# Softmax in an attention and MoE kernel on one Trainium2 core: chunked exponentials with the maximum as bias, and a new order at the start and in the pairs

## The chip, the cores and the metric

One core of one Trainium2 chip runs the whole program. The metric is the device time of one execution in microseconds (us). The engines are PE (TensorE matmul; PEld are its weight loads), DVE (VectorE), ACT (ScalarE), POOL (GpSimd) and SP (SyncE, which issues all the DMAs here). Each engine works through its own instructions strictly in the order in which they were issued, and waits on semaphores for the others.

## The reference

```python
# q, k, v: (8, 8, 576, 64); attention within chunks of 64 rows
scores = scale * np.matmul(q_c, k_c.transpose(0, 1, 2, 4, 3))      # scale = 1/8
scores = scores - np.max(scores, axis=-1, keepdims=True)
attn = np.exp(scores)
attn = attn / (np.sum(attn, axis=-1, keepdims=True) + 1e-09)
x = (attn @ v_c)  # put together as (4608 tokens, 512)
h = x @ w_in                                # 512 -> 2048
g = h * np.clip(h + 3.0, 0.0, 6.0) / 6.0
out = g @ w_out                             # 2048 -> 512
```

Everything is float32.

## The kernel before

**Blocks.** The 4608 tokens are nine blocks of NT = 512. Attention of a block is two objects `Attention(n, dp)`, each with four heads, laid out as tiles of 128 partitions by 2 x 8 x 64: sixteen pieces of 64 scores a row. `scores` are 64x64 matmuls into two PSUM banks (tile `two`). `soft` has five steps: 0 the row maximum (DVE, L172), 1 the subtraction of it from the scores (DVE, L174, PSUM to SBUF tile `e`), 2 the exponential over the whole tile (ACT, L176), 3 the row sum, the 1e-9 and the reciprocal (DVE, L178, L182, L183), 4 the normalisation (DVE, L185). `turn` transposes on PE, `turned` copies back (ACT, L202), `multiply` is the product with v (PE, L216), `multiplied` writes x (ACT, L228 or L233), and for the first three blocks DVE takes the low half (L234).

**Precision.** Each float32 product is three passes (L246 to L248) over a high and a low half of each operand. Weights come as 64-bit words, and each of sixteen weight tiles is converted: `u` (ACT, L105) from the high words, `r` (ACT, L106) from the low ones, a shift (DVE, L108) and an addition (DVE, L109), then the high half (ACT, L114, a cast) and the low half (DVE, L116).

**Stages.** First, block 0: its two attentions `b0` and `b1` are written out by hand among warm-up matmuls and the first conversions; b0's scores come in two halves `k` of four chunks. `part` are the twelve matmuls of block 0's first tile of h, in pieces. Then a loop over the sixteen tiles `ft` of block 0 converts tile ft + 2 while PE does `mm1(0, ft)` and `mm2` of two tiles earlier. Blocks 1 and 2 run the same way with converted weights. In this stage a table of slots, two per `ft`, places attention steps of later blocks.

**Pairs.** The other six blocks go in three pairs by a scheme with seven instead of eight block products. A pair has 112 slots of six 128x512 matmuls: 56 of the first product (eight columns p of seven products i in the order 1, 5, 6, 7, 2, 3, 4) and 56 of the second. After a slot's matmuls `tick` runs what `todo` holds for it, in order of rank: additions (L597), the gate (ReLU on ACT, L608, then DVE, L609), splits of operands into halves (`units`, `more`; ACT L446, DVE L447), attention steps of the next pair (`put_steady`). POOL does the two subtractions of each column (L617). Products 2, 3 and 4 go on accumulating in the PSUM banks of 1, 5 and 7, after the additions have read them.

What is issued when is an order written out by hand: the instructions of each engine stand in the order in which the Python code calls them.

Of the kernel before, what the change touches and what calls it, by code (L numbers as in the profile page):

```python
# [8 lines left out]
F32 = mybir.dt.float32  # L9
# [8 lines left out]
P = 128  # L18
# [21 lines left out]
FREE = 4 * NFT + 2 * (NFP + LAG + 1)  # L40


@with_exitstack
def tile_kernel(ctx: ExitStack, tc: tile.TileContext, qk_in, v_in, weights, out):
# [54 lines left out]
    def convert(ft, low_on):  # L99


        u = wsc.tile([P, 1024], I32, name="u")
        r = wsc.tile([P, 1024], I32, name="r")
        lo, hi = words[ft][:, :, 0], words[ft][:, :, 1]
        ACT.activation(out=u.bitcast(F32), in_=hi.bitcast(F32), func=AF.Prelu, scale=2.0 ** -112, alpha=2.0 ** 32)  # L105
        ACT.activation(out=r, in_=lo.bitcast(U32), func=AF.Copy, scale=2.0 ** -29)  # L106
        yield
        DVE.tensor_scalar(out=u, in0=u, scalar1=3, scalar2=None, op0=ALU.logical_shift_left)  # L108
        DVE.tensor_tensor(out=u, in0=u, in1=r, op=ALU.add)  # L109
        yield  # L110
        a = u.bitcast(F32).rearrange("p (m t) -> p m t", m=2)
        w[ft] = w_tile(ft, F32R)
        w_h[ft], w_l[ft] = w[ft][:, 0], w[ft][:, 1]
        ACT.copy(out=w_h[ft], in_=a)  # L114
        yield
        low_on.tensor_tensor(out=w_l[ft], in0=a, in1=w_h[ft].bitcast(F32), op=ALU.subtract)  # L116
        yield
# [4 lines left out]
    class Attention:  # L122
# [38 lines left out]
        def soft(self, step, k=None, a=None):  # L161

            every = slice(None)
            if k is None and a is None:
                flat, each = lambda t: t.rearrange("p a c t -> p (a c) t"), lambda t: t.rearrange("p a c -> p (a c)")
                src = step < 2 and flat(self.s)
            else:
                flat = each = lambda t: t[:, every if a is None else a, every if k is None else CHUNKS[k]]
                src = step < 2 and self.part[k]
# [3 lines left out]
            elif step == 1:  # L173
                DVE.tensor_tensor(out=flat(self.e), in0=src, in1=wide(self.m), op=ALU.subtract)  # L174
            elif step == 2:
                ACT.activation(out=flat(self.e), in_=flat(self.e), func=AF.Exp, scale=SCALE)  # L176
# [127 lines left out]
    with tc.tile_pool(name="ps_b", bufs=2, space=bass.MemoryType.PSUM) as ps_b:  # L304
        b0, b1 = [Attention(0, dp, lambda step, dp=dp: two_banks(ps_a if (dp, step) == (0, "o") else ps_b)) for dp in range(NDP)]
        b0.load_qk(parts=2)
        b1.load_qk(raw.tile([P, 2, 2, NB // 2, 2 * CH], F32, name="x"))
        b0.load_v()
        load_w(0)
        load_w(1)  # L310
        b1.load_v(gp.tile([P, 2, NB // 2, 2 * CH], F32, name="g"))
        a1[0].load_qk()
        load_w(2)
        load_w(3)

        c0, c1 = convert(0, DVE), convert(1, DVE)
# [26 lines left out]
        next(c0)  # L343
        warm_up(IDLE[4])
        b1.soft(3)
        next(c0)
        for a in range(2):
            b1.soft(4, a=slice(a, a + 1))
            b1.turn([a])
        finish()  # L350
        next(c1)
        h = ps_h.tile([P, NT], F32, name="h")

        def part(ct, which):
            o = slice(ct * P, (ct + 1) * P)
            x = xs[0, ct // 2][:, :, ct % 2]
            for k in which:
                PE.matmul(h, lhsT=(w_l if k == 2 else w_h)[0][:, 0, o], rhs=x[:, k % 2], start=ct == 0 and k == 0, stop=ct == 3 and k == 2)

        part(0, (0, 1))  # L360
        part(1, (0, 1))
        b1.turned([0])
        b1.turned([1])
        next(c1)
        next(c0)
        b1.multiply([0])
        b1.multiply([1])
        a1[0].scores()
        part(0, (2,))
        part(1, (2,))  # L370
        b1.multiplied([0])
        b1.multiplied([1])
        finish()
        next(c1)
        for k in range(3):
            part(2, (k,))
            part(3, (k,))
        next(c1)
# [151 lines left out]
    for ft in range(NFT):  # L530
# [5 lines left out]
        c = convert(ft + 2, DVE) if ft + 2 < NFT else None  # L536
        if c:
            next(c)
            next(c)
# [5 lines left out]
        if c:  # L545
            next(c)
            next(c)
# [41 lines left out]
    def at(slot, *f, rank=0):  # L589

        todo.setdefault(slot, []).extend((rank, g) for g in f)
# [7 lines left out]
    def put_steady(n, dp, at_):  # L599
        a = Attention(n, dp)  # L600
# [10 lines left out]
    def first_product(s, base, box):  # L611
# [3 lines left out]
        for p in range(NFP):  # L615
# [3 lines left out]
            for k, i in enumerate(ORDER_A):  # L619
# [18 lines left out]
                elif i == 7:  # L638
# [3 lines left out]
                    at(slot + 2, gate)  # L642
                elif i == 2:
                    at(slot + 1, *gated(gq(0, 0), ps))
                elif i in (3, 4):
# [3 lines left out]
                    at(slot + 2, gate)  # L649
                    if i == 3:  # L650
                        at(slot + 2, sub(out, out, gq(0, 0)), sub(t2[p // 2][:, p % 2], gq(1, 1), out))
# [69 lines left out]
    for s in range(NSUP):  # L721
        base = 2 * SLOTS * s
        if s + 1 < NSUP:
            for k in range(2 * NDP):
                put_steady(NSTD + 2 * s + 2 + k // 2, k % 2, base + (6, 23, 40, 78)[k])
# [7 lines left out]
        for k in range(4 * 7):  # L733
            at(base + SLOTS - 5 + int(1.75 * k), lambda k=k, unit=unit: unit(k), rank=1)
        if s + 1 < NSUP:
# [5 lines left out]
            for k in range(7):  # L741
                at(base + SLOTS + 44 + 2 * k, more, rank=1)
# [32 lines left out]
```

## Time and profile before

| | |
|---|---|
| median of 3 runs | 809.25 us (809.24 to 809.95) |
| profiled execution | 809.08 us |
| its span, first to last instruction | 807.2 us |
| granted TensorE clock | 0.999 |
| POOL busy | 65.0 us (8%) |
| DMA | 172.85 MB, mean 214 GB/s |
| chain that ended last | PE 86%, DVE 7%, ACT 4%, DMA 1% |

A profile row of the timeline has the start in us from the start of the span, the duration in us, engine, line, operation, output and inputs, shapes and the count of merged instructions; in brackets the engine's idle time before it and what ended that. A row of the groups has the shapes and count, then total busy us and mean ns of one, then idle us before it. Line numbers are those of the kernel before.

### The profile page before, as it was taken

The page shows a single profiled execution, that of the slowest core. Times are in us where ns is not written, and L with a number is a line of the kernel's source. Part 1 is how long each engine was busy: PE and PEld are TensorE (multiplying, and loading weights), DVE is VectorE, ACT ScalarE, POOL GpSimd, SP SyncE. Part 2 cuts the span into 40 slices and gives each one's busy share as a digit, 9 for nine tenths or more (in the row PEclk, how much of TensorE's full clock was granted, in tenths as well). Part 3 has the DMA queues.
Part 4 walks back from the last instruction along what each step waited for, and adds up shares of the span by engine and source line. Part 5 has one row for each costly group of instructions (what it writes and reads, how often), then busy time and mean ns, then how long its engine had stood idle before and what let it go on. Part 6 is the DMA issues. An engine that isn't in the chain of part 4 may idle for free.

```text
span 807.2 us, 13704 instructions
## 1 busy us (share of the span) xinstructions
PE 796.4 (99%) x5684; PEld 650.0 (81%) x5684; DVE 601.9 (75%) x771; ACT 366.9 (45%) x464; POOL 65.0 (8%) x55
## 2 busy tenths in 40 slices
PE   8999999999999999999999999999999999999997
PEld 5777888888888888888788888888788888888886
DVE  6889867897788682867888776778897856668941
ACT  5878644442453353344473433444634423347330
POOL 0000000000000000222110001222100012221000
PEclk9999999999999999999999999999999999999999
DMA  9980102968888753566556577665566665555463
GB/s 356 410 355 27 53 2 79 310 217 264 291 273 269 246 179 123 203 250 234 179 201 240 207 224 285 252 234 181 201 239 229 214 207 194 205 201 199 176 241 115
DMA packets 50157, 172.85 MB, mean 214 GB/s; under 512 B 4656, under 2 KB 16944, under 8 KB 39472
## 3 DMA queue, kind: packets, MB, share of 16 engines
q1 hardware_dynamic: 50096, 171.99, 60.3%
q8 instruction: 45, 0.74, 0.4%
q14 instruction: 16, 0.13, 0.0%
HBM read 133.17 MB, written 38.80 MB: 213 GB/s over the span
## 4 chain that ended last, share of the span: by engine, by line
PE 86%; DVE 7%; ACT 4%; DMA 1%; issue 1%; SPq 0%; DVEq 0%; ACTq 0%
PE acc L246 19%; PE acc L248 18%; PE acc L247 18%; PE h L246 8%; PE h L248 8%; PE h L247 8%; PE two L216 2%; PE two L154 2%; PE two L198 2%; DMA w<-w_in_out 1%; DVE u L109 1%; DVE u L597 1%; DVE g L609 1%; ACT r L106 1%; ACT u L105 1%
## 5 line engine op out<-in xcount | busy, mean ns | idle before, releaser
L246 PE MATMUL acc<-xop,ws 128*128 128x512 f32 x528 | 208.7, 395 | 0.5
L248 PE MATMUL acc<-xop,ws 128*128 128x512 f32 x528 | 205.7, 390 | 0.0
L247 PE MATMUL acc<-xop,ws 128*128 128x512 f32 x528 | 205.7, 390 | 0.0
L246 PEld LDWEIGHTS acc<-xop,ws 128*128 128x128 f32 x528 | 99.1, 188 | 24.2 <-DVE h L597 2.1
L248 PEld LDWEIGHTS acc<-xop,ws 128*128 128x128 f32 x528 | 99.1, 188 | 20.7
L247 PEld LDWEIGHTS acc<-xop,ws 128*128 128x128 f32 x528 | 99.2, 188 | 19.7
L447 DVE TENSOR_TENSOR xop<-g,xop 128x1024 fp32r<-128x1024 f32 x72 | 87.7, 1238 | 22.5 <-ACT xop L446 22.4
L446 ACT CAST xop<-g 128x1024 fp32r<-128x1024 f32 x72 | 73.2, 1051 | 38.7 <-PE acc L248 21.6
L617 POOL TENSOR_TENSOR g<-g 128x512 f32<-128x512 f32 x24 | 31.0, 1291 | 665.9 <-DVE g L609 665.9
L608 ACT ACTIVATE r<-acc,half 128x512 f32<-128x512 f32 x72 | 49.4, 686 | 71.9 <-DVE acc L597 71.9
L246 PE MATMUL acc<-g,w 128*128 128x512 f32 x192 | 76.3, 397 | 0.0
L246 PE MATMUL h<-x,w 128*128 128x512 f32 x188 | 74.2, 395 | 0.7 <-ACT w L114 0.7
L248 PE MATMUL acc<-g,w 128*128 128x512 f32 x192 | 74.9, 390 | 0.0
L247 PE MATMUL acc<-g,w 128*128 128x512 f32 x192 | 74.8, 390 | 0.0
L248 PE MATMUL h<-x,w 128*128 128x512 f32 x188 | 73.6, 391 | 1.2 <-DVE w L116 1.2
L247 PE MATMUL h<-x,w 128*128 128x512 f32 x188 | 73.2, 390 | 0.0
L609 DVE SCALAR_TENSOR_TENSOR g<-r,acc 128x512 f32<-128x512 f32 x72 | 49.0, 681 | 31.0 <-ACT r L608 31.0
L263 DVE SCALAR_TENSOR_TENSOR r<-r,h 128x512 f32<-128x512 f32 x48 | 32.7, 681 | 32.5 <-ACT r L262 32.5
L246 PE MATMUL h<-xop,ws 128*128 128x512 f32 x144 | 56.2, 391 | 0.0
L247 PE MATMUL h<-xop,ws 128*128 128x512 f32 x144 | 56.0, 389 | 0.0
L248 PE MATMUL h<-xop,ws 128*128 128x512 f32 x144 | 56.0, 389 | 0.0
L262 ACT ACTIVATE r<-h,half 128x512 f32<-128x512 f32 x48 | 32.8, 683 | 47.0 <-PE h L248 47.0
(86 smaller groups left out, 1163.9 us busy)
## 6 DMA issues: line engine op xcount, KB each, us to landing
ws<-b SPq DMA_DIRECT2D x42, 1024.0 KB, 4.8
ws<-a SPq DMA_DIRECT2D x24, 1024.0 KB, 4.9
ws<-a SPq DMA_DIRECT2D x24, 768.0 KB, 4.2
w<-w_in_out SPq DMA_DIRECT2D x16, 1024.0 KB, 18.0
qk<-qk_in SPq DMA_DIRECT2D x16, 1024.0 KB, 6.9
v<-v_in SPq DMA_DIRECT2D x17, 512.0 KB, 5.3
out_t<-o SPq DMA_DIRECT2D x32, 256.0 KB, 3.8
a<-hl SPq DMA_DIRECT2D x32, 256.0 KB, 3.0
```

Source lines behind the costliest of these rows:

```text
L154: PE.matmul(t[o, a, c if k is None else c % 4, :], lhsT=self.qk[rows, c // 4, 0, c % 4, o], rhs=self.qk[rows, c // 4, 1, c % 4, o], start= ...
L198: PE.transpose(out=self.tp[:, a, i], in_=self.e[:, a, 2 * i:2 * i + 2].rearrange("p c t -> p (c t)"), identity=ident)
L246: PE.matmul(ps, lhsT=a_h, rhs=b_h, start=first, stop=False, skip_group_check=more)
L247: PE.matmul(ps, lhsT=a_h, rhs=b_l, start=False, stop=False, skip_group_check=more)
L248: PE.matmul(ps, lhsT=a_l, rhs=b_h, start=False, stop=last, skip_group_check=more)
L262: ACT.activation(out=r, in_=h, func=AF.Relu, bias=half, scale=1.0 / 6.0)
L263: DVE.scalar_tensor_tensor(out=r, in0=r, scalar=1.0, in1=h, op0=ALU.min, op1=ALU.mult)
L446: ACT.copy(out=t[:, :, 0], in_=src)
L447: DVE.tensor_tensor(out=t[:, :, 1], in0=src, in1=t[:, :, 0].bitcast(F32), op=ALU.subtract)
L608: return (lambda: ACT.activation(out=r, in_=ps, func=AF.Relu, bias=half, scale=1.0 / 6.0), lambda: DVE.scalar_tensor_tensor(out=out, in0=r ...
L609: lambda: DVE.scalar_tensor_tensor(out=out, in0=r, scalar=1.0, in1=ps, op0=ALU.min, op1=ALU.mult))
L617: sub = lambda o, x, y: lambda: POOL.tensor_tensor(out=o, in0=x, in1=y, op=ALU.subtract)
```

## The change

The subtraction goes away. Step 1 of `soft` now multiplies the row maxima by -1/8 (ACT, 128x16 or 128x8 numbers), and step 2 is one ACTIVATE of 128x64 per chunk, straight from PSUM, with the column of negated maxima as the bias: sixteen where there was one, eight for each half of b0. At the start the first weight tile is loaded ahead of b0's v, the third ahead of block 1's q and k; a class `Convert` lets the six steps of a conversion be placed one by one; the low words of tile 0 are taken by POOL; and the steps, the pieces of `part` and block 1's scores come in another order. In the pairs, slots get fractional numbers: the whole part says after which slot, the fraction the rank. Attention steps of the pairs are given by a table instead of fixed distances, and the gates of products 7, 3 and 4 and POOL's subtractions get rank 0.1, behind the additions of rank 0. The slots of `units` and `more` are the same as before.

```diff
+STEADY = ((0.6, 6.6, 6.6, 7.5, 8.5, 12.5, 15.5, 17.6, 19.6), ..., (32.6, 38.6, 38.6, 39.5, 40.5, 44.5, 47.5, 49.6, 51.6), ...)
...
+        def words(self):
+            self.r = wsc.tile([P, 1024], I32, name="r")
+            lo = words[self.ft][:, :, 0].bitcast(U32)
+            if self.words_on:
+                self.words_on.tensor_scalar(out=self.r, in0=lo, scalar1=2.0 ** -29, scalar2=None, op0=ALU.mult)
+            else:
+                ACT.activation(out=self.r, in_=lo, func=AF.Copy, scale=2.0 ** -29)
...
             elif step == 1:
-                DVE.tensor_tensor(out=flat(self.e), in0=src, in1=wide(self.m), op=ALU.subtract)
+                ACT.mul(out=each(self.m), in_=each(self.m), mul=-SCALE)
             elif step == 2:
-                ACT.activation(out=flat(self.e), in_=flat(self.e), func=AF.Exp, scale=SCALE)
+                for i in range(2):
+                    for c in range(NB)[every if k is None else CHUNKS[k]]:
+                        s = self.s[:, i, c] if k is None else self.part[k][:, i, c - NB // 2 * k]
+                        ACT.activation(out=self.e[:, i, c], in_=s, func=AF.Exp, bias=self.m[:, i, c:c + 1], scale=SCALE)
...
+        load_w(0)
         b0.load_v()
-        load_w(0)
         load_w(1)
         b1.load_v(gp.tile([P, 2, NB // 2, 2 * CH], F32, name="g"))
+        load_w(2)
         a1[0].load_qk()
-        load_w(2)
         load_w(3)
-        c0, c1 = convert(0, DVE), convert(1, DVE)
+        c0, c1, c2 = Convert(0, POOL), Convert(1), Convert(2)
...
-        next(c0)
         for a in range(2):
             b0.soft(4, a=slice(a, a + 1))
             b0.turn([a])
+        c0.high()
+        c0.words()
+        b1.soft(0)
+        b1.soft(1)
+        c0.shift()
+        c0.add()
         warm_up(IDLE[3])
+        b1.soft(2)
         b0.turned([0])
         b0.turned([1])
         b0.multiply([0])
         b0.multiply([1])
-        b1.soft(0)
-        b1.soft(1)
-        b1.soft(2)
+        warm_up(IDLE[4])
+        c0.cast()
...
     def at(slot, *f, rank=0):
-        todo.setdefault(slot, []).extend((rank, g) for g in f)
+        todo.setdefault(int(slot // 1), []).extend((slot % 1 + rank, g) for g in f)
...
-        for k, f in ((-6, a.load_qk), (0, a.load_v), (0, a.scores), (1, a.tiles), (1, lambda: a.soft(0)), (2, lambda: a.soft(1)), (2, lambda: a.soft(2)), (8, lambda: a.soft(3)),
-                     (9, lambda: a.soft(4)), (12, a.transpose), (15, a.values)):
-            at(at_ + k, f, rank=2)
+        steps = (a.load_qk, a.load_v, lambda: (a.scores(), a.tiles()), soft(0), lambda: (a.soft(1), a.soft(2)), soft(3), soft(4), a.transpose, a.values)
+        for f, t in zip(steps, slots):
+            at(base + t, f)
...
                     at(slot + 1, add(acc[6], ps, u4), relu)
-                    at(slot + 2, gate)
+                    at(slot + 2, gate, rank=.1)
```

Where it moves instructions, first ACT at the start, from b0's exponentials on. In the rows `e` and `g` are the softmax tiles of b0 and b1, `two` a PSUM tile, `w` and `u` the weights. Before:

```order
L176 ACTIVATE e<-e 128x2x256 x2
L105 ACTIVATE u<-w_129 128x1024
L106 ACTIVATE r<-w_129 128x1024
L202 COPY e<-two 128x512 x2
L176 ACTIVATE g<-g 128x1024
L233 CAST x<-two 128x2x4x64 x2
L114 CAST w_349<-u 128x1024
L105 ACTIVATE u<-w_131 128x1024
```

ACT in the same place now:

```order
L192 ACTIVATE m<-m 128x2x4
L197 ACTIVATE e<-two,m 128x64 x8
L192 ACTIVATE m<-m 128x2x4
L197 ACTIVATE e<-two,m 128x64 x8
L112 ACTIVATE u<-w_127 128x1024
L192 ACTIVATE m<-m 128x16
L197 ACTIVATE g<-two,m 128x64 x16
L223 COPY e<-two 128x512 x2
L132 CAST w_372<-u 128x1024
L254 CAST x<-two 128x2x4x64 x2
L112 ACTIVATE u<-w_131 128x1024
```

b1's exponentials now stand ahead of the copy of b0's transposed tile, the cast of the first weights stands ahead of b0's x, and the low words (L106) are gone from ACT.

The second place is ACT in the conversion loop, at block 1's first attention (`r<-h` is the gate's ReLU). Before:

```order
L105 ACTIVATE u<-w_472 128x1024
L106 ACTIVATE r<-w_472 128x1024
L176 ACTIVATE e<-e 128x1024
L262 ACTIVATE r<-h,half 128x512
L114 CAST w_717<-u 128x1024
```

ACT in that place now:

```order
L112 ACTIVATE u<-w_506 128x1024
L120 ACTIVATE r<-w_506 128x1024
L192 ACTIVATE m<-m 128x16
L197 ACTIVATE e<-two,m 128x64 x16
L283 ACTIVATE r<-h,half 128x512
L132 CAST w_761<-u 128x1024
```

One exponential became a product and sixteen exponentials in the same place; what stands ahead and behind is the same.

The third place is DVE in the first pair, in the last two columns of the first product, from column p = 6 on (`u2`, `u4`, `h`, `acc` are additions, `g3` gates, `xop` splits, z and e attention's row sum and normalisation). Before, from that column's first addition:

```order
L597 TENSOR_TENSOR u2_3898<-h_3891,p1_3874 128x512
L597 TENSOR_TENSOR u4_3899<-acc_3882,u2_3898 128x512
L597 TENSOR_TENSOR h_3891<-acc_3900,u4_3899 128x512
L609 SCALAR_TENSOR_TENSOR g3_3206<-r_3909,h_3891 128x512
L609 SCALAR_TENSOR_TENSOR g3_3206<-r_3918,acc_3867 128x512
L597 TENSOR_TENSOR acc_3882<-acc_3882,u2_3898 128x512
L178 TENSOR_REDUCE z_3864<-e_3865 128x16
L182 TENSOR_SCALAR z_3864<-z_3864 128x16
L183 RECIPROCAL z_3864<-z_3864 128x16
L609 SCALAR_TENSOR_TENSOR g3_3206<-r_3927,acc_3882 128x512
L597 TENSOR_TENSOR acc_3900<-acc_3900,u2_3898 128x512
L185 TENSOR_TENSOR e_3865<-e_3865,z_3864 128x1024
```

DVE from the row sum on, now:

```order
L199 TENSOR_REDUCE z_4013<-e_4014 128x16
L203 TENSOR_SCALAR z_4013<-z_4013 128x16
L204 RECIPROCAL z_4013<-z_4013 128x16
L632 TENSOR_TENSOR u2_4092<-h_4085,p1_4070 128x512
L632 TENSOR_TENSOR u4_4093<-acc_4076,u2_4092 128x512
L632 TENSOR_TENSOR h_4085<-acc_4097,u4_4093 128x512
L645 SCALAR_TENSOR_TENSOR g3_3355<-r_4115,acc_4063 128x512
L645 SCALAR_TENSOR_TENSOR g3_3355<-r_4106,h_4085 128x512
L206 TENSOR_TENSOR e_4014<-e_4014,z_4013 128x1024
L632 TENSOR_TENSOR acc_4076<-acc_4076,u2_4092 128x512
L632 TENSOR_TENSOR acc_4097<-acc_4097,u2_4092 128x512
L645 SCALAR_TENSOR_TENSOR g3_3355<-r_4124,acc_4076 128x512
```

The row sum moved from behind the column's first accumulator addition to ahead of its first addition, and the two accumulator additions now stand together ahead of their gates.

More of the change, by code (lines that the diff above doesn't have):

```diff
@@ L97, in load_w, with __init__, high, shift @@
         words[ft] = t.rearrange("p (n t) -> p n t", t=2)
[L99 to L117, printed above, removed]
+    class Convert:
+        def __init__(self, ft, words_on=None):
+            self.ft, self.words_on = ft, words_on
+        def high(self):
+            self.u = wsc.tile([P, 1024], I32, name="u")
+            hi = words[self.ft][:, :, 1]
+            ACT.activation(out=self.u.bitcast(F32), in_=hi.bitcast(F32), func=AF.Prelu, scale=2.0 ** -112, alpha=2.0 ** 32)
+        def words(self):
[5 more added lines that the diff above has]
+                ACT.activation(out=self.r, in_=lo, func=AF.Copy, scale=2.0 ** -29)
+        def shift(self):
+            DVE.tensor_scalar(out=self.u, in0=self.u, scalar1=3, scalar2=None, op0=ALU.logical_shift_left)
+        def add(self):
+            DVE.tensor_tensor(out=self.u, in0=self.u, in1=self.r, op=ALU.add)
+        def cast(self):
+            self.a = self.u.bitcast(F32).rearrange("p (m t) -> p m t", m=2)
+            t = w[self.ft] = w_tile(self.ft, F32R)
+            w_h[self.ft], w_l[self.ft] = t[:, 0], t[:, 1]
+            ACT.copy(out=t[:, 0], in_=self.a)
+        def low(self):
+            DVE.tensor_tensor(out=w_l[self.ft], in0=self.a, in1=w_h[self.ft].bitcast(F32), op=ALU.subtract)
     def two_banks(p):
@@ L349, in tile_kernel, with part @@
             b1.turn([a])
+        c0.low()
         finish()
-        next(c1)
+        b1.turned([0])
+        b1.turned([1])
+        c1.shift()
+        c1.add()
+        c2.high()
+        c2.shift()
         h = ps_h.tile([P, NT], F32, name="h")
-        def part(ct, which):
+        def part(ct, k):
             o = slice(ct * P, (ct + 1) * P)
             x = xs[0, ct // 2][:, :, ct % 2]
[L357 to L365, printed above, removed]
+            PE.matmul(h, lhsT=(w_l if k == 2 else w_h)[0][:, 0, o], rhs=x[:, k % 2], start=ct == 0 and k == 0, stop=ct == 3 and k == 1)
+        for k in (0, 2):
+            part(0, k)
+            part(1, k)
         b1.multiply([0])
         b1.multiply([1])
-        a1[0].scores()
-        part(0, (2,))
-        part(1, (2,))
         b1.multiplied([0])
         b1.multiplied([1])
+        c1.cast()
         finish()
[L374 to L378, printed above, removed]
+        c1.low()
+        c2.words()
+        part(0, 1)
+        part(1, 1)
+        for k in (0, 2, 1):
+            part(2, k)
+            part(3, k)
+            if k == 2:
+                a1[0].scores()
     ps_o = pool("ps_o", 4, space=bass.MemoryType.PSUM)
@@ L535, in tile_kernel @@
         over = []
[L536 to L539, printed above, removed]
+        c = None
+        if ft + 2 < NFT:
+            c = Convert(ft + 2) if ft else c2
+            if ft:
+                c.high()
+                c.words()
+                c.shift()
+            c.add()
         gt = gate(h)
@@ L545, in tile_kernel @@
         if c:
-            next(c)
-            next(c)
+            c.cast()
+            c.low()
         if len(pending) >= LAG:
@@ L731, in unit @@
             next(box["units"])
-        for k in range(4 * 7):
-            at(base + SLOTS - 5 + int(1.75 * k), lambda k=k, unit=unit: unit(k), rank=1)
+        for k, t in enumerate(UNITS):
+            at(base + SLOTS + t, lambda k=k, unit=unit: unit(k))
         if s + 1 < NSUP:
@@ L739, in more @@
                 next(box["x"])
-            for k in range(7):
-                at(base + SLOTS + 44 + 2 * k, more, rank=1)
+            for t in MORE:
+                at(base + SLOTS + t, more)
         first_product(s, base, box)
```

24 lines of the change are left out of this document (14 added, 10 removed).

## Prediction

> **What bounds the kernel now.** I read the page first, then the stretches, then the timeline of each engine where TensorE is not full.
>
> ```profile
> PE 796.4 (99%) x5684; PEld 650.0 (81%) x5684; DVE 601.9 (75%) x771; ACT 366.9 (45%) x464; POOL 65.0 (8%) x55
> ```
> ```profile
> 10.00:20.00 10.00, 9.22 (x140) 7.68 (x134) 9.43 (x15) 7.33 (x10) 0.00 (x0) 1.00 1.02 412
> 100.00:200.00 100.00, 100.00 (x804) 82.20 (x803) 76.62 (x119) 42.14 (x58) 0.00 (x0) 1.00 0.54 172
> ```
> Behind the time in a row of the stretches stand busy us of PE, PEld, DVE, ACT and POOL, the clock, the DMA share and GB/s. From 100 to 200 us TensorE is busy throughout at clock 1.00, and no matmul is removed by the change. So DVE and ACT time is worth nothing by itself; the change can win or lose only where TensorE waits for them. The timeline of PE shows three such places: the first 33 us, the conversion of the weights up to 65 us, and the last column of each pair's first product.
>
> **The start.** The other engines' rows there:
>
> ```profile
> 6.30 0.69 DVE L172 TENSOR_REDUCE m<-two 128x8 f32<-128x512 f32 x1 [5.44 <-PE two L154]
> 8.96 1.46 DVE L178 TENSOR_REDUCE z<-e 128x8 f32<-128x512 f32 x2
> 10.95 1.29 DVE L185 TENSOR_TENSOR e<-e,z 128x512 f32<-128x512 f32 x2
> 12.16 1.22 DVE L172 TENSOR_REDUCE m<-two 128x16 f32<-128x1024 f32 x1
> ```
> ```profile
> 12.66 1.14 ACT L105 ACTIVATE u<-w 128x1024 f32<-128x1024 f32 x1 [2.96 <-DMA w<-w_in_out]
> 14.76 1.05 ACT L202 COPY e<-two 128x512 f32<-128x512 f32 x2
> 28.46 1.05 ACT L114 CAST w<-u 128x1024 fp32r<-128x1024 f32 x1 [1.03 <-DVE u L109]
> 29.93 1.13 ACT L105 ACTIVATE u<-w 128x1024 f32<-128x1024 f32 x1
> ```
> The first weights land at 12.66. Moved ahead of b0's v (0.5 MB, at 412 GB/s 1.3 us) they land near 11.4; v then lands near 12.7 and is needed only after the copy that stood at 14.76, so it costs nothing. The third weights change places with block 1's q and k (1 MB each, 2.6 us): those then land about when the third weights did, some 22 us, and their scores stand behind b1's product with v, later than 25 us here. b1's scores now wait for b0's first eight exponentials to leave their PSUM bank, 9.0 instead of about 8.9, ahead of warm-up matmuls that nothing needs: no cost.
>
> The price that decides is one exponential of 128x64 with a pointer as bias, out of PSUM. No row has it. The nearest:
>
> ```profile
> L608 ACT ACTIVATE r<-acc,half 128x512 f32<-128x512 f32 x72 | 49.4, 686 | 71.9 <-DVE acc L597 71.9
> L202 ACT COPY e<-two 128x1024 f32<-128x1024 f32 x16 | 16.2, 1011 | 22.5 <-PE two L198 22.4
> L202 ACT COPY e<-two 128x512 f32<-128x512 f32 x2 | 1.0, 574 | 0.0
> L74 ACT ACTIVATE warm<-half 128x1 f32<-128x1 f32 x1 | 0.2, 203 | 0.0
> ```
> ```profile
> 387.27 0.69 ACT L608 ACTIVATE r<-h,half 128x512 f32<-128x512 f32 x1 [2.90 <-DVE h L597]
> 387.86 0.68 ACT L608 ACTIVATE r<-acc,half 128x512 f32<-128x512 f32 x1
> ```
> An element costs (1011 - 574)/512 = 0.85 ns. The gate's ReLU has the same operands (PSUM in, pointer bias): 686 - 448 x 0.85 = 305 ns for 64 columns, and 387.27 to 387.86 shows that the next starts 0.59 after it, 0.59 - 0.38 = 0.21 for 64. I take 0.20 from start to start. Ends: 0.31 (no overlap) and 0.10 (574 ns copies follow each other by 1.05 - 0.57 = 0.48, so 0.48 - 0.38). The multiplication of the maxima by -1/8 is 0.21 by the 128x1 row, and 0.04 to hand on.
>
> The Trainium skill, "ScalarE: Activation LUTs", section "What ACT_TABLE_LOAD costs", gives 280 ns + 0.833 ns a column with a pointer bias, overlapping by 93 ns: an estimate of 0.24 for 64. For the 512-column ReLU it gives 707 and 614 ns where the rows have 686 and 590, so I keep the trace's; by the page 48 exponentials add 1.9 us to the sum.
>
> Now b0: maximum ends 6.99, product 7.24, eight exponentials from 7.28 to 8.88, second product, eight more until 10.84 (before, 9.7). Row sum 0.7: 11.55; the two small steps, 0.53 from the end of 8.96 + 1.46 to 10.95: 12.1; normalisation 1.29, then b1's maximum 1.22: 14.5; product, sixteen exponentials of 0.20: 18.0. Only then does ACT come to b0's transposed copy, which stood at 14.76: b1's exponentials are now in front of it.
>
> The first tile's low words go from ACT (1.14) to POOL, at just that time:
>
> ```profile
> L617 POOL TENSOR_TENSOR g<-g 128x512 f32<-128x512 f32 x24 | 31.0, 1291 | 665.9 <-DVE g L609 665.9
> 338.04 1.29 POOL L617 TENSOR_TENSOR t<-g 128x512 f32<-128x512 f32 x1
> 338.35 1.01 DVE L182 TENSOR_SCALAR z<-z 128x16 f32<-128x16 f32 x1
> ```
> The last row is a DVE step of 128x16 that stands still until POOL's subtraction is over (339.33). POOL's new 128x1024 reads as many elements as these two 512s: 1.3 us, between 0.65 (half) and 2.6 (twice). From 11.4 it holds POOL until 12.7, over b0's 1e-9 step, due at 11.6: 1.2 us later (0 to 2.4), and the copy at 19.2.
>
> From that copy to the fourth tile's first activation ACT needed 29.93 - 14.76 = 15.2 us. Out of this go b1's exponential (1.06) and about the 1.03 that the cast waited at 28.46, since third and second tile are now shifted earlier: 13.1. So 32.3, which is 2.4 later.
>
> **The conversion.** The chain of waits runs through ACT and DVE until 65.25, with this hole:
>
> ```profile
> 50.51 1.22 DVE L172 TENSOR_REDUCE m<-two 128x16 f32<-128x1024 f32 x1
> 54.21 1.22 DVE L174 TENSOR_TENSOR e<-two,m 128x1024 f32<-128x1024 f32 x1
> ```
> ```profile
> 50.80 1.11 ACT L106 ACTIVATE r<-w 128x1024 int32<-128x1024 uint32 x1
> 55.46 1.06 ACT L176 ACTIVATE e<-e 128x1024 f32<-128x1024 f32 x1 [3.55 <-DVE e L174]
> 56.42 0.67 ACT L262 ACTIVATE r<-h,half 128x512 f32<-128x512 f32 x1
> ```
> ```profile
> 58.08 0.50 PE L246 MATMUL h<-x,w 128*128 128x512 f32 x1 [0.21 <-ACT w L114]
> 59.34 0.50 PE L248 MATMUL h<-x,w 128*128 128x512 f32 x1 [0.53 <-DVE w L116]
> 65.25 0.50 PE L248 MATMUL h<-x,w 128*128 128x512 f32 x1 [0.19 <-DVE w L116]
> ```
> ACT stands idle 3.55 us for the subtraction. With none, the maximum is there at 51.73 (50.51 + 1.22), ACT is free at about 51.85, the product is done at 52.05, sixteen exponentials fill the hole to 55.27, and the ReLU starts there instead of at 56.42: 1.15 earlier, and casts and low halves behind it too. TensorE, which waits for these at 58, 59 and 65, then comes out 2.4 - 1.15 = 1.25 later than before. Between 65 and 280 us it waits for nothing; sixteen exponentials lengthen ACT's line by 2.3 us an attention and shorten DVE's by 1.2, and ACT is 42% busy there: no cost.
>
> **The pairs.** TensorE's waits in the last column of a first product (pair one, then three):
>
> ```profile
> 397.59 0.39 PE L248 MATMUL acc<-xop,ws 128*128 128x512 f32 x1
> 398.11 0.50 PE L246 MATMUL acc<-xop,ws 128*128 128x512 f32 x1
> ...
> 399.14 0.39 PE L247 MATMUL acc<-xop,ws 128*128 128x512 f32 x1
> 399.37 0.39 PE L248 MATMUL acc<-xop,ws 128*128 128x512 f32 x1
> 399.85 0.50 PE L246 MATMUL acc<-xop,ws 128*128 128x512 f32 x1
> ```
> ```profile
> 724.51 0.40 PE L248 MATMUL acc<-xop,ws 128*128 128x512 f32 x1
> 724.99 0.50 PE L246 MATMUL acc<-xop,ws 128*128 128x512 f32 x1
> ```
> ```profile
> 397.97 1.22 DVE L447 TENSOR_TENSOR xop<-g,xop 128x1024 fp32r<-128x1024 f32 x1
> 399.10 0.69 DVE L597 TENSOR_TENSOR h<-acc,u 128x512 f32<-128x512 f32 x1
> ```
> A step is 0.23 (399.14 to 399.37); 0.52 and 0.48 lose 0.29 and 0.25, and the slower first step after a wait 0.1 each: 0.75 in pair one, as much in two, 0.36 in three, 1.9 us together. The matmul at 399.85 waits for the addition of 399.10, which stands behind a split that stands behind the chain of gates. Now both additions of a slot go ahead of the gates, the third attention's row sum comes four slots earlier within the pair, its normalisation two, and its product with v (1.1 us on TensorE) moves ahead of the two matmuls. I lay the additions at least 0.4 us ahead of their matmuls in all three pairs. In return the row sum's tail now falls into POOL's two subtractions of column five, behind the exponentials: by the 1.01 row some 0.85 late, and the matmul behind the next addition waits about 0.45, in two pairs. So 1.0 of the 1.9 goes; ends 1.9 and -0.5 (all waits kept, the new ones added). The exponentials hold ACT for 3.2 us, and ReLUs queue behind them. Worst is the second attention: a slot is six steps, 1.36 us; counted from the end of its slot of scores, they run from 2.6 to 5.8, the ReLU and gate that free the first bank (0.69 each, two of each ahead) end at 7.6, and the bank is wanted by the matmul seven slots on, at 9.3: hidden, with 1.7 to spare, and at 0.31 a piece just used up.
>
> **Sum.** +2.4 - 1.15 - 1.0 = +0.3 on the profiled 809.08 (span 807.2 and 1.9 around it): 809.4. The median of the runs is 0.17 above the profiled one: 809.5.
>
> **Rivals.** *Dear exponentials.* Of them 48 lie on the chain (32 at the start, 16 in the hole), so 0.01 more is 0.5 us. At 0.24, 811.4; at 0.31, 814.8, pairs aside. It decides from 0.23 on. For it: a 64-column instruction is mostly fixed cost, and no row goes below 128x512 but one 203 ns; against it: the ReLU's 0.59. This is where the page's estimate would lie. 0.25.
> *Cheap exponentials.* At 0.10 the chain would come 3.5 us before the old one; then TensorE itself bounds, and it wins its start (about 0.8) and the waits of 58 to 65 (0.93 by their brackets, 1.5 with the slow steps): 805.9 with the pairs. Decides from 0.17 down. For it the 0.48 of the copies. 0.17.
> *POOL out of the way.* If the word step is short, or starts behind the normalisation, the start is 1.2 better, and with all pair waits gone the time is 807.4. 0.11.
> *Nothing to see.* The terms cancel as I sum them, or DVE's relief lies beside a full TensorE: 807.6 to 810.9. 0.45, my forecast.
>
> **How the numbers follow.** A measurement of this kernel tells about 0.2% (1.6 us) from no change. Faster by more: 0.17 + 0.11 = 0.28. Slower by more: 0.25 and 0.02 for a longer POOL step, 0.27. Within: 0.45. The range takes in most of the cheap and the dear case up to 0.27, 806.2 to 812.8; the forecast's own is 807.6 to 810.9.
>
> **What would show it.** In the new profile: 128x64 exponentials 0.20 apart; b0's copy (L223) near 19 us instead of 14.76; a DVE 128x16 step stretched under POOL near 11.6; the fourth tile's first activation near 32.3; ACT without the 3.55 hole and TensorE's waits at 58 to 60 down to about 0.4; the last column of the third pair without a wait, the first two pairs with a new one two slots before the column ends. Wrong would be: exponentials outside 0.17 to 0.23, a start that does not move by 2 to 3 us, or waits of TensorE between 65 and 280 us.

## The result and the profile after

The changed kernel takes 815.05 us (median of 6 runs, 814.69 to 816.2) against 809.24 before: a ratio of 1.0073, 95% interval 1.006 to 1.0086. It is 5.8 us slower, where I forecast 809.5 and gave 812.8 as the upper end.

The busy times of the page after (engine, us, share of the span, instructions), to be held against the first row that the prediction shows (from here on a row's line numbers are those of the kernel whose trace it is from):

```profile
PE 799.5 (98%) x5684; PEld 652.1 (80%) x5684; DVE 582.6 (72%) x752; ACT 409.1 (50%) x751; POOL 71.3 (9%) x56
```

TensorE has the same 5684 matmuls. DVE lost 19 us, ACT got 42 more, and neither says anything of the time: where TensorE waits does. Held against each other matmul by matmul, the later start of the same matmul after than before is:

| place (us before) | later by | predicted up to here |
|---|---|---|
| fourth tile's first activation on ACT (29.93) | 3.42 | 2.4 |
| behind the hole (59.34) | 2.35 | 1.25 |
| up to 232 | 2.35 | 1.25 |
| end of block 1 (232 to 263) | 4.85 | 1.25 |
| end of pair one's first product (402.53) | 6.02 | |
| end of pair two's (570.05) | 6.89 | |
| end of pair three's (727.42) | 6.31 | 0.3 |
| end of the span | 5.8 | 0.3 |

**The price.** The group of the exponentials after (total us, mean ns of one), and one run of sixteen in the timeline of ACT:

```profile
L197 ACT ACTIVATE e<-two,m 128x64 f32<-128x64 f32 x272 | 57.8, 361 | 0.6
```
```profile
55.23 0.20 ACT L192 ACTIVATE m<-m 128x16 f32<-128x16 f32 x1
55.47 3.39 ACT L197 ACTIVATE e<-two,m 128x64 f32<-128x64 f32 x16
58.64 0.80 ACT L283 ACTIVATE r<-h,half 128x512 f32<-128x512 f32 x1
```

The row of sixteen lasts 3.39 us and one lasts 0.361, so they start (3.39 - 0.361)/15 = 0.202 us apart: the 0.20 of the prediction. So an attention's exponentials hold ACT for 3.4 us where the one exponential before took 1.06.

**The start.** Timelines of ACT, DVE, POOL and PE after:

```profile
11.51 1.13 ACT L112 ACTIVATE u<-w 128x1024 f32<-128x1024 f32 x1 [0.85 <-DMA w<-w_in_out]
15.25 3.39 ACT L197 ACTIVATE g<-two,m 128x64 f32<-128x64 f32 x16
18.41 1.19 ACT L223 COPY e<-two 128x512 f32<-128x512 f32 x2
25.16 1.07 ACT L223 COPY g<-two 128x512 f32<-128x512 f32 x2 [1.11 <-issue]
33.35 1.14 ACT L112 ACTIVATE u<-w 128x1024 f32<-128x1024 f32 x1
```
```profile
11.41 0.17 DVE L203 TENSOR_SCALAR z<-z 128x16 f32<-128x16 f32 x1
11.91 1.93 DVE L206 TENSOR_TENSOR e<-e,z 128x512 f32<-128x512 f32 x2
```
```profile
11.56 2.86 POOL L118 TENSOR_SCALAR r<-w 128x1024 int32<-128x1024 uint32 x1 [9.81 <-DMA w<-w_in_out]
```
```profile
14.38 2.35 PE L88 MATMUL h<-ident 128*128 128x256 bf16 x20
19.17 1.67 PE L237 MATMUL two<-e,v 64*64 64x64 f32 x64 [2.44 <-ACT e L223]
20.77 3.43 PE L88 MATMUL h<-ident 128*128 128x256 bf16 x20
```

b0's copy stands at 18.41, later than before by 3.65, since b1's pieces are in front of it. Behind it comes what I had not reckoned with: TensorE is idle for 2.44 us, and then the same twenty warm-up matmuls take 3.43 us instead of 2.35. Four stretches of 3.41 us show why (time, then busy us of PE, PEld, DVE, ACT and POOL, granted clock, DMA share, GB/s); they are cut where the granted clock of this trace changes:

```profile
5.95:9.36 3.41, 1.56 (x57) 1.18 (x57) 1.94 (x3) 2.51 (x13) 0.00 (x0) 1.00 0.99 407
9.36:12.77 3.41, 3.41 (x71) 2.74 (x62) 2.11 (x5) 2.43 (x8) 1.21 (x1) 0.50 1.03 418
...
16.18:19.60 3.42, 0.98 (x34) 0.68 (x35) 1.69 (x2) 3.42 (x15) 0.00 (x0) 1.00 1.04 423
19.60:23.01 3.41, 3.41 (x63) 2.68 (x53) 3.31 (x7) 3.07 (x6) 0.00 (x0) 0.50 1.02 408
```

The clock falls to 0.50 twice, each time for 3.41 us and behind a stretch in which TensorE was busy for less than half; before, it was 1.00 all along there. The first fall costs nothing up to the copy, which stands at 18.43 in experiment 7 without it. Behind the second, b1's transposes come late, and ACT waits 1.11 us for its second copy.

**The hole** is filled (55.23 to 58.64 above, no idle time), and 1.07 of the 3.42 come back.

**231 us.** ACT's timeline at the end of block 1, before and then after, SyncE's issues of the output transfers, before and after, and the matmuls that wait after:

```profile
226.83 0.59 ACT L292 COPY o<-acc 128x512 f32<-128x512 f32 x1 [2.64 <-DMA out_t<-o]
227.31 1.07 ACT L176 ACTIVATE e<-e 128x1024 f32<-128x1024 f32 x1
228.27 1.04 ACT L420 CAST hl<-a 128x1024 fp32r<-128x1024 f32 x1
229.21 0.62 ACT L266 CAST g<-r 128x512 fp32r<-128x512 f32 x1
```
```profile
230.21 0.59 ACT L313 COPY o<-acc 128x512 f32<-128x512 f32 x1 [3.62 <-DMA out_t<-o]
230.94 3.39 ACT L197 ACTIVATE e<-two,m 128x64 f32<-128x64 f32 x16
234.10 1.16 ACT L449 CAST hl<-a 128x1024 fp32r<-128x1024 f32 x1
235.04 0.74 ACT L287 CAST g<-r 128x512 fp32r<-128x512 f32 x1
```
```profile
222.85 4.93 SPq L293 DMA_DIRECT2D out_t<-o x4
226.86 4.29 SPq L314 DMA_DIRECT2D out_t<-o x4
```
```profile
235.84 0.51 PE L267 MATMUL acc<-g,w 128*128 128x512 f32 x1 [1.04 <-ACT g L287]
236.56 0.51 PE L268 MATMUL acc<-g,w 128*128 128x512 f32 x1 [0.22 <-DVE g L289]
```

ACT stands still behind an output copy that waits for its buffer. Before, 1.07 us of exponential followed it, and the gate's cast ended at 229.83, 2.4 us ahead of the matmul of 232.25 that needs it. Now product and pieces take 3.4 us, and from the copy's start to that of the cast it is 4.83 us instead of 2.38. And the copy itself comes 1.0 late against TensorE (3.38, of which 2.39 is what TensorE has lost by then), because the transfer that frees its buffer is issued 4.0 later. In SyncE's queue it stands behind the stores of split operands (`b<-hl`, `b<-w`), and those come late behind the pieces of the attention at 203 us, as experiment 10 shows. The two, 2.45 and 1.0, are more than the 2.4 to spare, and the second product waits for the cast.

**The pairs.** TensorE's waits in pair one, and the DVE and POOL rows beside the first of them:

```profile
346.19 1.06 PE L219 MATMUL two<-ident,e 128*128 128x128 f32 x8 [0.39 <-DVE e L206]
393.38 0.50 PE L267 MATMUL acc<-xop,ws 128*128 128x512 f32 x1 [0.48 <-DVE u L632]
398.09 1.06 PE L219 MATMUL two<-ident,e 128*128 128x128 f32 x8 [0.34 <-DVE e L206]
```
```profile
344.11 1.93 DVE L206 TENSOR_TENSOR e<-e,z 128x1024 f32<-128x1024 f32 x1
390.76 1.00 DVE L203 TENSOR_SCALAR z<-z 128x16 f32<-128x16 f32 x1
396.72 1.22 DVE L206 TENSOR_TENSOR e<-e,z 128x1024 f32<-128x1024 f32 x1
```
```profile
343.68 1.29 POOL L653 TENSOR_TENSOR g<-g 128x512 f32<-128x512 f32 x1 [9.79 <-DVE g L645]
345.04 2.13 POOL L653 TENSOR_TENSOR t<-g 128x512 f32<-128x512 f32 x1
```

The same three come in pair two, at 514.59, 561.80 and 566.51. Each loses some 0.5 to 0.65 us, the slow first step included. The one at 393.38 is the wait that I predicted (the row sum's tail, 1.00 instead of 0.17, under POOL). The two at the transposes I did not see. One attention's normalisation, at 344.11, now falls beside POOL's subtractions and takes 1.93 us instead of 1.24. The one ahead of 398.09 takes its plain 1.22, with POOL idle: it stands behind the additions and gates that the row sum's tail has held up, and in experiment 6 this wait and that of 393.38 go together. That it follows from the first is likely, but no run takes it alone.

### The profile page after: what moved, and what is told of

It is laid out like the page before. It is cut to its first block, busy times and chain, and to the rows that moved or that the text cites. A ratio compares the mean times of both kernels' runs of the same rounds, so it can differ in the third digit from the quotient of the medians.

```text
span 813.0 us, 13941 instructions
## 1 busy us (share of the span) xinstructions
PE 799.5 (98%) x5684; PEld 652.1 (80%) x5684; DVE 582.6 (72%) x752; ACT 409.1 (50%) x751; POOL 71.3 (9%) x56
## 4 chain that ended last, share of the span: by engine, by line
PE 81%; DVE 8%; ACT 8%; issue 1%; DMA 1%; SPq 1%; POOL 0%; DVEq 0%; ACTq 0%; POOLq 0%
PE acc L267 17%; PE acc L268 17%; PE acc L269 17%; PE h L267 8%; PE h L269 8%; PE h L268 8%; ACT e L197 2%; PE two L237 2%; PE two L172 2%; PE two L219 2%; DVE e L206 1%; DVE g L645 1%; DVE z L199 1%; ACT u L112 1%; ACT r L644 1%
## 5 line engine op out<-in xcount | busy, mean ns | idle before, releaser
L476 DVE TENSOR_TENSOR xop<-g,xop 128x1024 fp32r<-128x1024 f32 x72 | 89.6, 1264 | 21.5 <-ACT xop L475 21.5
L644 ACT ACTIVATE r<-acc,half 128x512 f32<-128x512 f32 x72 | 47.6, 695 | 48.2 <-DVE acc L632 46.1
L197 ACT ACTIVATE e<-two,m 128x64 f32<-128x64 f32 x272 | 57.8, 361 | 0.6
```

Of the source, the lines that this page charges most:

```text
L197: ACT.activation(out=self.e[:, i, c], in_=s, func=AF.Exp, bias=self.m[:, i, c:c + 1], scale=SCALE)
L476: DVE.tensor_tensor(out=t[:, :, 1], in0=src, in1=t[:, :, 0].bitcast(F32), op=ALU.subtract)
L644: return (lambda: ACT.activation(out=r, in_=ps, func=AF.Relu, bias=half, scale=1.0 / 6.0), lambda: DVE.scalar_tensor_tensor(out=out, in0=r ...
```

## The experiments

Two theories at first. **Q**: the sixteen pieces are the loss, wherever ACT's line leads to TensorE's next wait, and the missing subtraction is a gain. **O**: the new orders and slots are the loss. Kernel "before" was run beside each set, 809.22 to 809.33 us in the median.

**1. All orders new, old softmax.**

```diff
-ACT.mul(m, -SCALE); 16 x ACT.activation(128x64, bias=m)
+DVE.tensor_tensor(e, s, m, subtract); ACT.activation(128x1024)
```

> The changed kernel with the old softmax put back everywhere (subtraction on DVE, one exponential per tile); order of the start, rank of the gates and slots of the pairs stay new. Theory Q (ACT's queue): what was lost is the ACT time of sixteen pieces, 3.4 us instead of 1.06, at the places where ACT's line leads to the next wait of TensorE; the new orders cost little. Then the start is within 0.7 us of the kernel before, the wait of 1.2 us near 234 us is gone, and the pairs win 1.0 to 1.9: 807.3 to 809.0 us. Theory O (order): the loss lies in the new start, where b1's exponentials stand ahead of b0's copy and TensorE idles, and in the new slots: 811 us or more.

809.63 (ratio 1.0003, 0.9994 to 1.0012). It lies between the two. The new softmax (pieces in, subtraction out) carries 5.4 of the 5.8 us; and no wait is left at 234 us. But the three waits of each pair are there just the same (342.04, 389.28 and 393.99 in pair one): they belong to the slots.

**2. The new softmax alone, orders and slots of before.**

> The kernel before with nothing changed but the softmax (negated maximum as bias, sixteen exponentials of 64). Theory Q: start about 2.4 late, less 1.1 won back in the conversion, 2.2 at the end of block 1 and 0.5 to 1.5 in the pairs: 813 to 815 us. Theory O: the old order of the start hides most of it, and the old slots have no new wait: 809 to 811.5 us.

821.74 (1.0153, 1.0139 to 1.0167). Dearer than either theory had it: 2.4 us later at 65 us, 3.0 more between 228 and 241, and 6.9 in the pairs, where TensorE waits 0.95, 0.56, 0.29 and 0.89 us in pair one and as much in pair two, slow first steps not counted.

**3. The pairs' new slots and ranks alone.**

> The kernel before with the new slots and the rank of gates in the pairs alone; old softmax, old start. Theory Q: the column-end waits of the first products (0.75, 0.75 and 0.36 us) go and little comes in their place: 807.3 to 808.4 us. Theory O: the slots themselves make the new waits (row sum ahead of the column's first addition, POOL beside the normalisation): 809.3 to 811 us.

810.64 (1.0018, 1.0009 to 1.0026): O is right for the slots, +1.36 us. TensorE's waits in pair one:

```profile
342.26 1.06 PE L204 MATMUL two<-ident,e 128*128 128x128 f32 x8 [0.45 <-DVE e L191]
...
389.48 0.50 PE L252 MATMUL acc<-xop,ws 128*128 128x512 f32 x1 [0.49 <-DVE u L605]
394.18 1.07 PE L204 MATMUL two<-ident,e 128*128 128x128 f32 x8 [0.31 <-DVE e L191]
```

**4. The late output copy moved** behind the next slot's gate in the changed kernel:

```diff
+            if op and et == NET - 1:
+                put(slot + 1, copy_out, 30)
```

> The changed kernel, with the fourth output copy of blocks 0 and 1 issued one slot later, behind the exponentials on ACT instead of ahead of them. If the waits of TensorE from 234 to 240 us come from the exponentials standing behind a copy that itself waits 3.6 us for its buffer: those waits go, 812.5 to 813.1 us. If 3.4 us of exponentials alone are enough to make the gate late: 814.4 to 815.2 us.

813.93 (1.0053, 1.0041 to 1.0066). The waits at 235 to 240 go, but the copy's PSUM bank is now free too late, and TensorE waits 1.28 us for it at 232.81. So 1.1 us came back; what the pieces do there is left to experiments 10 and 11.

**5. Tile 0's low words on ACT** (`Convert(0)` for `Convert(0, POOL)`).

> The changed kernel, with the first tile's low words on ACT again instead of POOL. If POOL's 2.86 us step is what slowed the normalisation beside it (two of 1.93 us start to end 0.64 later than in the kernel before), then ACT, which is idle there until the maximum is out near 15, takes the words at no cost, b0's copy comes 0.6 to 0.8 us earlier (17.6 to 17.8) and the time is 814.2 to 814.5. If ACT's line is what matters (its 1.1 us lands ahead of the sixteen exponentials), the copy is no earlier and the time is 815.0 to 815.6.

814.75 (1.0062, 1.0048 to 1.0075): by time between the two. In the trace the two normalisations are back at 1.29 and the copy at 17.49, 0.92 earlier; of this 0.65 is left in the pairs and 0.55 at the last matmul. POOL's step costs under 1 us.

**6. One exponential per instruction**, in the changed kernel, straight from PSUM (the bias is the first chunk's maximum; the maxima of the others are left out):

```diff
+ACT.activation(out=flat(self.e), in_=flat(self.s), func=AF.Exp, bias=self.m[:, 0, 0:1], scale=SCALE)
```

> The changed kernel with one exponential over all chunks of an instruction, with the first chunk's maximum as bias (it leaves out the maxima of the other chunks). No subtraction and no sixteen pieces: 1.1 us of ACT where the changed kernel has 3.4. Theory Q (the sixteen pieces hold ACT's line up): nearly all of the 5.8 us goes and the subtraction's gain shows: start back to the 0.65 us loss of the run with the old softmax, less about 1.2 in the hole and 1.2 at the start, no wait near 234 us, the three pair waits of the new slots stay: 806.5 to 808.5. Rival, the subtraction was worth nothing where it stood: 809.3 to 810.0. Rival, the new orders carry the loss: 811 or more.

804.14 (0.994, 0.9928 to 0.9952), better than Q expected, and 10.9 us better than the changed kernel. The wait at 235 us is gone, and so are two of the three in each pair. Dropping the subtraction is the gain that it was hoped to be; cutting the exponential in sixteen turns it over.

**7. TensorE's idle stretch filled**: `IDLE` from (0, 4, 16, 20, 20) to (0, 4, 16, 40, 4), in the changed kernel.

> The changed kernel with twenty more warm-up matmuls ahead of b0's transposed copy and sixteen fewer behind it. If TensorE's idle 2.4 us there is what brings its granted clock to 0.84 from 10 to 30 us, and the slow warm-up and transposes (3.43 us for 20 where the kernel before has 2.36) hold up b1's, then the clock is back near 1.0, the fourth tile's first activation comes about 1 us or more earlier (32.3 instead of 33.35) and the time is 813.7 to 814.3. If the clock falls for another reason, or the matmuls there are not on the chain, 814.8 to 815.3.

813.32 (1.0051, 1.0038 to 1.0064), and the stretches:

```profile
10.00:20.00 10.00, 8.45 (x133) 7.13 (x127) 7.30 (x10) 6.74 (x25) 2.86 (x1) 1.00 1.03 418
20.00:30.00 10.00, 9.03 (x182) 6.11 (x173) 9.78 (x14) 9.22 (x13) 0.00 (x0) 1.00 1.02 405
```

b0's copy stands where it stood (18.43), but the clock is 1.00 and everything behind it 1.65 us earlier to the end. So 1.7 us of the loss lies in this stretch. Sixteen warm-up matmuls are gone behind it too; that it is the clock, and not these or the idle time, experiment 9 shows.

**8. The new softmax in block 1 alone**, in the kernel before.

> The kernel before with the new softmax only in the two attentions of block 1, whose first lies in the hole of 3.55 us where ACT waits for the subtraction during the conversion. Theory Q: there the pieces take the hole and not ACT's line, so the waits at 58 and 59 us shrink by about 1.1 and nothing else moves: 807.9 to 808.5. Rival: the gain is given back at once, because the casts behind then wait for ACT or the weights: 809.0 to 809.6. Rival: the pieces cost more there too, as at 65 us where chunks alone came 2.4 late: 810 or more.

807.90 (0.9983, 0.9975 to 0.9992), as Q expected. ACT's hole of 3.55 us is filled (pieces from 52.16, ReLU at 55.33 instead of 56.42), and TensorE's waits of 0.21 and 0.53 us there are gone.

Where ACT waits for DVE, sixteen pieces are a gain of 1.3 us.

**9. The old slots under the changed kernel.**

> The changed kernel with the pairs' slots and ranks of the kernel before. The prediction held the pieces' delay in a pair to be hidden, with 1.7 us to spare, whatever the slots: then about 1 us less than the changed kernel, since the new slots' own waits (three a pair, 1.6 us, against 0.55) go: 813.5 to 814.5. Rival: without the new slots the queue behind the pieces reaches TensorE (chunks alone in the kernel before showed waits of 1.1, 0.7, 0.5 and 1.1 us in a pair): 3 to 4 us a pair in two pairs or more, 820 to 823.

820.02 (1.0136, 1.0122 to 1.015): the rival. My step that the pieces' delay in the pairs is hidden holds only with the new slots; with the old ones TensorE waits in pair one as here:

```profile
363.81 0.50 PE L267 MATMUL acc<-xop,ws 128*128 128x512 f32 x1 [0.96 <-DVE g L642]
371.51 0.51 PE L267 MATMUL acc<-xop,ws 128*128 128x512 f32 x1 [0.54 <-DVE h L630]
391.97 0.50 PE L267 MATMUL acc<-xop,ws 128*128 128x512 f32 x1 [0.31 <-ACT p L667]
405.04 0.50 PE L267 MATMUL acc<-xop,ws 128*128 128x512 f32 x1 [0.90 <-DVE u L630]
```

So the slots cost 1.4 us by themselves, and with the pieces the kernel is 5 us faster for them.

This trace also parts the clock from the idle time, since its start is the same. TensorE is idle just as long there, from 16.6 to 19.0 us, and has the same twenty warm-up matmuls behind it, but the clock stays at 1.00: they take 2.36 us, and TensorE's first matmul behind `part` comes at 29.16 instead of 30.86. The fourth tile's first activation is at 31.64 instead of 33.35. The 1.7 us are the clock's, and the idle time by itself costs next to nothing. The stretches of 3.41 us here fall otherwise:

```profile
14.20:17.62 3.42, 2.36 (x22) 1.87 (x20) 2.43 (x3) 2.75 (x14) 0.06 (x1) 1.00 1.02 407
17.62:21.03 3.41, 2.03 (x73) 1.87 (x74) 2.42 (x5) 3.41 (x10) 0.00 (x0) 1.00 1.02 417
```

**10. The old softmax in one attention of the changed kernel**, `(self.n, self.dp) != (3, 0)` keeps the pieces:

> The changed kernel with the old softmax (subtraction, one exponential) in the one attention whose sixteen pieces run at 231 to 234 us behind the late output copy. If the pieces alone hold up the gate's cast there, the waits of 1.04, 0.5 and 0.3 us at 235 to 240 go and with them what followed, 2.2 us: 812.7 to 813.2. If the late copy, which waits for an output buffer until 230.2, holds it up by itself: 814.2 to 815.2.

814.23 (1.0054, 1.0041 to 1.0067). I had named the wrong attention: this one runs at 203 us. Yet the wait of 1.04 is nearly gone (its matmul comes at 235.25, 0.46 instead of 0.23 behind the one before), while the waits of 0.2 behind it stay. ACT's copy and SyncE's transfers:

```profile
229.62 0.59 ACT L320 COPY o<-acc 128x512 f32<-128x512 f32 x1 [2.65 <-DMA out_t<-o]
225.62 4.94 SPq L321 DMA_DIRECT2D out_t<-o x4
```

The transfers are issued 1.2 us earlier than after, though TensorE is 0.4 later here, and the copy waits 2.65 as before and not 3.62. So the pieces at 203 us make the copy late, and that is 1.0 of the loss at 231: between 230 and 250 us TensorE loses 1.3 here and 2.2 after.

**11. The same for the right one**, `(4, 0)`.

> The changed kernel with the old softmax in the one attention whose sixteen pieces run at 231 to 234 us behind the late output copy (the run before this one changed the attention of 203 us). If the pieces alone hold up the gate's cast, the waits of 1.04, 0.5 and 0.3 us at 235 to 240 go: 812.7 to 813.2. If the copy that waits for an output buffer until 230.2 does it by itself: 814.2 to 815.2.

812.59 (1.0034, 1.0021 to 1.0046). No wait is left between 68 and 343 us, although the copy comes even later; ACT's timeline:

```profile
231.17 0.59 ACT L320 COPY o<-acc 128x512 f32<-128x512 f32 x1 [4.00 <-DMA out_t<-o]
231.65 1.06 ACT L204 ACTIVATE e<-e 128x1024 f32<-128x1024 f32 x1
233.55 0.62 ACT L294 CAST g<-r 128x512 fp32r<-128x512 f32 x1
```

So without these pieces even a later copy costs nothing, and with them it costs: the pieces of this attention are worth 2.5 us by the medians (1.6 by the two profiled executions), some 1.0 of it through the late copy.

**12. The old softmax in block 0 alone**, in the changed kernel (32 of its 288 exponentials; the 48 of the expectation is a slip).

> The changed kernel with the old softmax in the two attentions of block 0 alone (48 instead of 272 of its exponentials less). If the pieces at the start are the largest part of the loss, the start is that of the run with the old softmax everywhere, the hole at 54 us stays filled (1.1), the 2.3 us at 231 and the 1 us of the pairs stay: 811 to 812. If the start's loss is given back later in any case: 814 to 815.

811.58 (1.0031, 1.002 to 1.0042). The pieces at the start, with the clock that falls behind them, cost 3.5 us: at 59 us TensorE is 1.7 ahead of before, where after it is 2.35 late.

**13. Towards a faster kernel: the gates behind the additions** (rank 0.1), in the kernel before.

> The kernel before with one thing of the change: in the pairs' first product the gate steps of a slot stand behind the additions (rank 0.1); the slots of the attentions, of the units and of the last steps stay. If the order of gates and additions makes the waits in the last column (0.3 and 0.25 us in pairs one and two, 0.25 in pair three, with slow first steps 1.9 in all), they go: 807.4 to 808.2. If they come from the attention's steps that lie there, or the gates then hold up something else: 809.0 to 809.8.

808.00 (0.9985, 0.9976 to 0.9994): of the change's slots, this part gains 1.2 us. If the two parts of the slots add, the table of the attentions costs 1.36 + 1.2, about 2.6.

**14. That and block 1's pieces.**

> The kernel before with the new softmax in the two attentions of block 1 alone (807.9 by itself) and the gate steps behind the additions. If both gains are independent: 806.2 to 807.0. If the gates' rank gives nothing: 807.7 to 808.2. If it takes something: above 808.4.

807.22 (0.9973, 0.9962 to 0.9984). Of 1.3 + 1.2 the two together give 2.0.

**15. One exponential in the kernel before**, with the row's largest score over all chunks of the instruction as bias (for b0, each half's).

> The kernel before, its orders and slots, with a softmax that needs neither subtraction nor pieces: the largest score of a partition's row over all its chunks serves as bias of one exponential per instruction (the sum is the same softmax, but for the 1e-9 that is added to a sum of smaller terms). Theory Q (no subtraction is a gain, the pieces are the loss; orders and slots are not needed without them): the start and the hole give what they gave with one pass in the changed kernel (1.7 us at 65 us, and 0.65 more since the old order is not late there), the pairs keep the old waits: 804.0 to 805.5, against 804.14 with the new orders. Rival: the new orders and slots are part of that gain: 806 to 808.

807.45 (0.9974, 0.9964 to 0.9984): the rival. With the old start ACT waits until 12.69 for the first weights, so a shorter softmax finds nothing to do there; experiment 17, with the new start, bears this out.

**16. That with the gates behind.**

> As the one before, and the gate steps of a slot behind the additions. If the last column's waits of 1.4 to 1.9 us come from that order: 802.4 to 804.0. If not: as the one before, 804.0 to 805.5.

806.50 (0.9963, 0.995 to 0.9977). Another 0.95 us, but not the 802.4 to 804.0 that I expected.

**17. The new start, the old slots with the gates behind, and one exponential.**

> The changed kernel's start and conversion, one exponential per instruction with the largest score of the partition's row as bias (but for the 1e-9 the same softmax), the slots of the kernel before in the pairs, and the gate steps behind the additions. If the start's order carries the 3 us between 804.1 (new orders and slots) and 807.4 (old ones), and the slots cost 0.55 twice against 0.25 twice: 803.2 to 804.2. If the slots carry it: 805.5 to 807.

804.30 (0.994, 0.9926 to 0.9954). The start's order carries the difference: 804.30 against 806.50. It is as good as experiment 6 with a bias that covers every chunk. The softmax is the same but for the 1e-9, which weighs more in a chunk whose maximum lies far below the row's. ACT's timeline at the start (18.41 for the copy after, 33.35 for the last row):

```profile
12.98 1.11 ACT L201 ACTIVATE g<-two,m 128x1024 f32<-128x1024 f32 x1
13.99 1.06 ACT L227 COPY e<-two 128x512 f32<-128x512 f32 x2
...
28.55 1.14 ACT L112 ACTIVATE u<-w 128x1024 f32<-128x1024 f32 x1
```

## Why the prediction was wrong, step by step

By the runs, the 5.8 us are: pieces at the start 3.5 (12), of which the clock 1.7 (7, 9); pieces at 231 us 2.5 (11); slots 1.4 (3); the hole -1.3 (8); and the new start order by itself about 809.63 - 809.28 - 1.36 = -1.0 (1 less 3). That makes 5.1. The remaining 0.7 is open: the parts were taken out of different kernels, and the start's clock, which changes between executions of several of these kernels, moves a median by as much. The start order is the least sure: at 30.82 us TensorE is 0.6 ahead in the trace of experiment 12, which has the old softmax and the new order there, but 0.8 late in that of experiment 1, its slowest execution (810.84).

- **Price of an exponential, 0.20 us: right** (0.202). The Trainium skill's 0.24 ("ScalarE: Activation LUTs", "What ACT_TABLE_LOAD costs") is not borne out. My rival of dear exponentials had its number, 814.8, near the outcome by a wrong reason: that is luck.
- **b0's copy, 19.2 predicted, 18.41 measured.** The step that a DVE step stands still until POOL is over failed: the 1e-9 step slipped in at 11.41, 0.15 us ahead of POOL, and the normalisation ended ahead of POOL, only 0.64 slower. POOL's step itself was 2.86 us, above my upper end of 2.6. Without it the copy stood at 17.49 (5) where I had 18.0.
- **"From that copy to the fourth tile's first activation", 13.1: failed**; it took 14.94. I took the stretch from the trace of before, in which the clock was 1.00 throughout. That the later copy leaves TensorE without work, and that its clock then falls, was no term of the sum. With the clock at 1.00 the stretch took 13.4 (9). The 1.84 too little, less the 0.8 by which the copy came early, is the +1.0 of the +3.42 where I had +2.4.
- **The hole, -1.15: right** (-1.07, and -1.3 by itself).
- **"Between 65 and 280 us it waits for nothing", ACT 42% busy, "no cost": failed**; it cost 2.5 us, as large a miss as that of the pairs. That TensorE does not wait before the change says nothing of how much slack is left, and 42% is a mean over 100 us. The slack of 2.4 us was to be read on ACT's line ahead of the gate's cast, and the output copy that waits 2.64 us at 226.83 was in the trace of before. That pieces elsewhere make this copy later still, by way of SyncE's queue, was to be seen only by following the stores too.
- **Pairs, -1.0: failed**; +1.5 in the trace (4.85 to 6.31), a miss of 2.5. The gain of the gates' rank is real (-1.2, experiment 13, where I had up to 1.9), and pair three's wait went as predicted. But I priced one new wait under POOL a pair and there are three. I held the third attention's row sum against POOL's pairs of subtractions of 1.3 us, but not another attention's normalisation, and not the third's own against its transposes.
- **The pieces' delay in the pairs "hidden, with 1.7 to spare": held** with the new slots, which I had not credited with it: with the old ones the kernel is 5 us slower (9).
- **Range.** I gave it to the price of an exponential, the one number that no row had. What decided were places at which the known price came to bear.

## What to carry to other kernels

Splitting one long instruction into many short ones is paid wherever that engine's line is short of slack just once, not on average: walk the line ahead of every wait of the bounding engine, above all behind a transfer's wait, before calling a longer instruction hidden. A bias that is one number per partition for the whole tile takes the same subtraction away in one instruction (with all else as in the kernel before, 807.45 against 821.74), so look for a coarser bias that the mathematics allows before paying for the exact one. When a step ahead of TensorE gets longer, fill the stretch that it leaves idle: the idle time itself cost next to nothing here, the clock that fell behind it 1.7 us.

## What the runs showed of the hardware

- The granted clock changed only at cuts 3.41 us apart. After a stretch of 3.41 us in which TensorE's matmuls were busy for 0.98 or 1.56 us it was 0.50 for the whole next stretch, and twenty warm-up matmuls took 3.43 us instead of 2.35. In the starts of all these traces (to 27 us), wherever the cut of the stretches is known, 13 stretches had such a fall behind them, with 0.98 to 1.74 us of matmuls; those with 1.77 and more had none, and neither had one with 1.72 (experiment 8). So about half of a stretch is the limit here.
- Where the cut lies differs between executions, and so the same kernel does not always lose its clock. The 2.44 us of idle time lie within one stretch after (0.98 us of matmuls); in experiment 9 the cut at 17.62 halves them (2.36 and 2.03), and the clock stays. Of experiment 5's five executions two took 813.3 and 813.6 us at a mean clock of 1.000, three 814.75 to 815.37 at 0.995 to 0.998.
- The Trainium skill, "TensorE: Matmul & The Clock Gate", Part 1, has the half rate and a free-running window of about 3.4 us, and the trace agrees with both. It puts the fall behind a window that was idle; here one that was up to half busy was enough.
- POOL's multiplication of 128x1024 numbers from uint32 to int32 took 2.86 us beside DVE's normalisation; what it takes alone, no run shows.
- Who gives way between DVE and POOL: in the pairs the normalisation of 344.11 ended 1.07 us after POOL's first subtraction (344.97) and POOL's second took 2.13 us instead of 1.29, as if each had waited for the other. At the start it was not so: two normalisations begun inside POOL's step ended (13.84) before it did (14.42), only 0.64 late.
